# Reordering the SP queue of a fused attention and two-expert kernel: weight stores behind newer loads, raw keys and queries behind the moves

## The chip, the core and the metric

The kernel runs on one core of a Trainium2 chip. The metric is the device time of one execution in microseconds (us); it is stated as the median of several runs. The engines are TensorE (PE in the rows; PEld is its weight load), VectorE (DVE), ScalarE (ACT), GpSimd (POOL) and SyncE (SP). SP does no arithmetic here: it issues transfers (DMAs), in the order of its queue, and when the next one has to wait for a semaphore, everything behind it on SP waits too. ScalarE's queue issues a few transfers as well.

## What is computed

Four batches of eight heads of attention (576 positions, head dimension 64), with a threshold, then two experts, of two dense layers each, on the 2304 x 512 result:

```python
scores = scale * np.matmul(q, k.transpose(0, 1, 3, 2))
thresh = np.max(scores, axis=-1, keepdims=True) - tau
scores = np.where(scores >= thresh, scores, -1000000000.0)
attn = softmax(scores)
x = (attn @ v), heads side by side
h = x @ w_in;  x = (s * relu(h)**2 + b) @ w_out        # first expert, d_ff 2048
h = x @ w2_in; out = mish(h) @ w2_out                  # second expert, d_ff 2048
```

The expert weights arrive as 64-bit floating point numbers and are converted on the chip. Keys, queries and values arrive as 32-bit numbers.

## The kernel before, in words

**Attention.** The 32 heads are worked off in 16 pairs; a pair has nine score tiles. `attention` (L422) goes through all 144 tiles: `scores` (L326) computes a tile's scores on TensorE from the pair's Q, KH and KL tiles, VectorE takes minimum and threshold, ScalarE the exponential; `weights_t` (L373) transposes the tile on TensorE (T, L380), ScalarE copies the transpose from PSUM (te, L391), and `products_v` (L394, L406 and L409) multiplies te with the values (pv), with a lag of some seven tiles.

**Preparing the next pair.** While pair p is computed, at its score tiles 2 and 4, `prep_qk` (L298) prepares the keys and then the queries of pair p + 1. `raw_t` (L264) transposes the raw tile on TensorE (tpk, tpq) and at its end calls `load_raw` (L234), which loads the raw keys or queries of pair p + 2 into the same raw tile with two DMAs on SP (L254 for 512 positions, L255 for the last 64); there is one raw tile for keys and one for queries, so this load waits until the transposes have read it. `parts` (L278) splits the transpose into hi (ScalarE, L282) and lo (VectorE, L283), of which there is one tile each, used by keys and queries in turn. Then SP issues the moves (L303), six for keys (four of KH, two of KL) and four for queries, which copy the parts into the tiles of the pair. `self.moved` remembers the last move. The first pair goes through `prep_first` (L305).

**Weights of the first expert.** `split_all` (L162) runs the 32 pieces of the first expert's weights through a software pipeline: a step traces one new piece's load and advances the older pieces by one stage each, the oldest first. `split_w` (L47) loads the raw piece with one DMA of 512 KB (L60, into one of four raw slots; it is queued on SP behind `self.moved`), ScalarE scales its high words in place (L66), VectorE assembles the 32-bit number (L68 to L70), ScalarE rounds it to hi (L73), and VectorE or GpSimd takes the rest (L74). The result stands in one of the five slots of the ring. When a piece is finished, `store` (L193) writes it to DRAM (L195), from where the later batches reload it (L494). A ring slot is free again when its store has been read out and the matmuls that use it are done.

**The mixed order.** After the first pairs, `run` (L774) traces attention and `moe1` (L483, the first expert, batch by batch, matmuls on L502) alternately, by estimated work done; attention is traced with a higher priority there. During batch 0 of the first expert a step of `split_all` is taken every fourth yield. The final order on each engine is laid when the program is built, by priority and by simulated times, under the dependencies and the order edges: `issue_after(x)` lets what is traced in it be issued only behind x on x's queue, without waiting for x to finish.

Of the kernel before, what the change touches and what calls it, by code (L numbers as in the profile page):

```python
# [8 lines left out]
F32 = mybir.dt.float32  # L9
# [10 lines left out]
class Fused:  # L20
# [26 lines left out]
    def split_w(self, src, hi, lo, pool, tags, kw):  # L47

        nc = self.nc
        i = self.nd
        self.nd += 1
        n = src.shape[1] * src.shape[2] // 2
        raw = pool.tile([P, n, 2], I32, tag=tags[0], name=f"wraw{i}", **kw)
        with self.tc.issue_after(self.moved):
            nc.sync.dma_start(raw.rearrange("p (c f) w -> p c (f w)", c=src.shape[1]), src)  # L60
        low, high = raw[:, :, 0], raw[:, :, 1]
        hf = high.bitcast(F32)
        yield
        yield
        a = pool.tile([P, n], I32, tag=tags[1], name=f"wa{i}")
        self.tc.keep_in_program_order(nc.scalar.activation(hf, hf, AF.Copy, scale=2.0 ** -112))  # L66
        yield
        nc.vector.tensor_scalar(a, high, 3, None, op0=ALU.logical_shift_left)  # L68
        nc.vector.scalar_tensor_tensor(a, low, 29, a, op0=ALU.logical_shift_right, op1=ALU.bitwise_or)
        nc.vector.scalar_tensor_tensor(a, high, -0x80000000, a, op0=ALU.bitwise_and, op1=ALU.bitwise_or)  # L70
        yield
        af = a.bitcast(F32).rearrange("p (c f) -> p c f", c=src.shape[1])
        nc.scalar.copy(hi, af)  # L73
        (nc.gpsimd if self.s2p else nc.vector).tensor_tensor(lo, af, hi.bitcast(F32), op=ALU.subtract)  # L74
# [102 lines left out]
    def w1_pieces(self, layer, qf, i):  # L177

        nc = self.nc
        key = (layer, qf, i)

        def piece():
            u = self.w1[key] = self.ring.tile([P, 2, 4, 128], F32R, tag="ring", name=f"wp{layer}_{qf}_{i}")
            if layer == 0:
                r0, c0, w = 0, qf * 512 + i * 128, self.w_in
            else:
                r0, c0, w = qf * 512, i * 128, self.w_out
            src = w[r0:r0 + 512, 2 * c0:2 * c0 + 256].rearrange("(c p) f -> p c f", c=4)  # L190
            return src, u[:, 0], u[:, 1], store

        def store():  # L193
            dst = self.w1s[key] = self.dram.tile([P, 2, 4, 128], F32, name=f"w1_{layer}_{qf}_{i}")
            nc.sync.dma_start(dst, self.w1[key].bitcast(F32))  # L195

        return [piece]

    def busy(self, out, n):

        w = out.shape[1]
        for _ in range(n):
            ins = self.nc.tensor.matmul(out, self.ones[:, :128], self.ones[:, :w], start=True, stop=True)
            self.tc.keep_in_program_order(ins)
# [59 lines left out]
    def raw_t(self, pr, n):  # L264
        nc = self.nc
        raw = self.raws.pop((pr, n))
        tp = self.s_tile(f"tp{n}{pr}")

        for c, o in ((4, 192), (0, 256), (1, 384), (2, 512), (3, 640), (4, 768)):
            rows = raw[:, c].rearrange("p h d -> p (h d)")  # L270
            if c < 4:
                nc.tensor.transpose(tp[:, o:o + 128], rows, self.ident)
            else:
                nc.tensor.matmul(tp[:, o:o + 64], rows, self.ident[:, 0:64], start=True, stop=True)
        self.load_raw(pr + 1, n)
        return tp

    def parts(self, pr, n, tp, tags):  # L278
# [19 lines left out]
    def prep_qk(self, pr, n):  # L298

        hi, lo = self.parts(pr, n, self.raw_t(pr, n), ("hi", "lo"))  # L300
        for h in range(2):
            for dst, src in self.moves(pr, n, h, hi, lo):
                self.moved = self.nc.sync.dma_start(dst.bitcast(F32), src.bitcast(F32)).ins  # L303

    def prep_first(self, busy):  # L305


        nc = self.nc
        tps = [self.raw_t(0, n) for n in "kq"]
        busy(6)  # L310
        (kh, kl), (qh, ql) = (self.parts(0, n, tp, tags) for n, tp, tags in
                              zip("kq", tps, (("hi", "lo"), ("e", "e"))))
        k0, k1, k2 = self.moves(0, "k", 0, kh, kl)
        q0, q1 = self.moves(0, "q", 0, qh, ql)
        nc.scalar.copy(k0[0], k0[1].bitcast(F32))
        nc.gpsimd.tensor_copy(k1[0], k1[1].bitcast(F32))
        nc.gpsimd.tensor_copy(k2[0], k2[1].bitcast(F32))
        nc.scalar.copy(q0[0], q0[1].bitcast(F32))
        nc.vector.tensor_copy(q1[0], q1[1].bitcast(F32))
        for n, hi, lo in (("k", kh, kl), ("q", qh, ql)):  # L320
            for dst, src in self.moves(0, n, 1, hi, lo):
                nc.sync.dma_start(dst.bitcast(F32), src.bitcast(F32))
# [613 lines left out]
```

## Time and profile before

| | us |
|---|---|
| median of 3 runs | 1150.73 |
| lowest and highest of them | 1149.34, 1155.08 |
| the profiled execution, its own time | 1157.07 |
| its span, first to last instruction | 1155.3 |
| TensorE busy | 1091.3 |
| VectorE busy | 798.6 |
| ScalarE busy | 619.2 |
| GpSimd busy | 251.6 |

The profile is of one execution. Its first part gives busy time per engine. The view of stretches splits that by time; the waits name who stood idle and which instruction ended the wait; the timeline lists instructions with start and duration, and behind a square bracket the idle time before one and what ended it. A row of SP gives the time in which SP issued a transfer, not the transfer's own.

### The profile page before, as it was taken

Reading aid. Unit: us, or ns where it says so; the run is one execution under the profiler, and the core shown is the slowest. Engines: PE = TensorE matmul, PEld = TensorE weight load, DVE = VectorE, ACT = ScalarE, POOL = GpSimd, SP = SyncE. Lnnn points to the kernel's source line nnn. Section 1 sums busy time; section 2 is a strip of 40 time slices with the busy share of each in tenths; the row PEclk is TensorE's granted clock in tenths of the full one; section 3 lists DMA queues with packets and bytes.
Section 4 is the critical chain, followed back from the end, with each engine's and each line's share of the span. In section 5 each row is a group of like instructions: output and inputs, shape, how many; then the busy total and the mean of one; then the engine's idle time right before and its main releaser. Section 6 shows DMA issues by size and latency. Waiting matters only on the chain.

```text
span 1155.3 us, 21402 instructions
## 1 busy us (share of the span) xinstructions
PE 1091.3 (94%) x7964; PEld 1023.6 (89%) x7964; DVE 798.6 (69%) x1747; ACT 619.2 (54%) x1153; POOL 251.6 (22%) x305
## 2 busy tenths in 40 slices
PE   7887899888899999999999999989999999999998
PEld 6766688778688999899998889989999999999998
DVE  6978666868697567786687667643787377834783
ACT  4656576637466765666675557633454144513351
POOL 4533333334143334332442311100000000000000
PEclk9999899999999999999999999989999999999999
DMA  7466464665758866988684899975999999996783
GB/s 159 102 153 158 134 203 134 213 161 206 218 156 275 259 196 221 268 269 264 232 269 146 329 365 369 381 282 204 361 378 346 315 409 369 363 332 250 270 301 115
DMA packets 141591, 292.70 MB, mean 253 GB/s; under 512 B 52848, under 2 KB 78960, under 8 KB 133168
## 3 DMA queue, kind: packets, MB, share of 16 engines
q1 hardware_dynamic: 134256, 286.91, 72.6%
q10 hardware_dynamic: 7232, 4.43, 1.5%
q8 instruction: 63, 1.03, 0.4%
q14 instruction: 40, 0.33, 0.1%
HBM read 201.85 MB, written 66.58 MB: 232 GB/s over the span
## 4 chain that ended last, share of the span: by engine, by line
PE 60%; DMA 5%; DVE 3%; ACT 2%; issue 1%; SPq 0%; DVEq 0%; ACTq 0%
PE o L747 15%; PE y L502 12%; PE h L502 10%; PE qY L613 6%; PE qX L613 4%; PE qV L613 4%; PE S L342 3%; PE T L380 2%; PE pv L409 2%; DMA wi<-wsi 2%; DMA w<-w 1%; DMA wraw<-in_moe_w_out_dram 1%; PE pv L406 1%; DVE e L357 1%; DMA crawo<-in_moe_w_out_dram 1%
## 5 line engine op out<-in xcount | busy, mean ns | idle before, releaser
L747 PE MATMUL o<-wo,hl 128*128 128x256 f32 x1512 | 177.7, 279 | 0.0
L747 PEld LDWEIGHTS o<-wo,hl 128*128 128x128 f32 x1512 | 177.4, 188 | 0.0
L367 POOL TENSOR_SCALAR e<-e,st 128x576 f32<-128x576 f32 x128 | 130.1, 1029 | 199.8 <-DVE st L362 155.4
L502 PE MATMUL h<-xh,w 128*128 128x288 f32 x768 | 166.8, 302 | 4.0 <-DMA w<-w 3.8
L502 PE MATMUL y<-gh,w 128*128 128x288 f32 x768 | 164.1, 301 | 2.8 <-DVE y L549 2.0
L346 DVE TENSOR_SCALAR_CACHE_REDUCE ns<-S 128x576 f32<-128x576 f32 x144 | 107.7, 752 | 45.9 <-PE S L342 45.5
L357 DVE SCALAR_TENSOR_TENSOR e<-ns,st,e 128x576 f32<-128x576 f32 x128 | 115.2, 903 | 35.0 <-ACT e L353 34.0
L391 ACT COPY te<-T 128x576 f32<-128x576 f32 x144 | 91.3, 634 | 79.7 <-PE T L385 64.6
L502 PEld LDWEIGHTS h<-xh,w 128*128 128x128 f32 x768 | 127.5, 191 | 5.1 <-DMA w<-w 4.1
L502 PEld LDWEIGHTS y<-gh,w 128*128 128x128 f32 x768 | 126.7, 190 | 3.7 <-DVE y L549 2.2
L353 ACT ACTIVATE e<-ns,st 128x576 f32<-128x576 f32 x128 | 98.8, 775 | 56.5 <-DVE ns L346 50.0
L526 POOL TENSOR_TENSOR gl<-rr,gh 128x288 fp32r<-128x288 f32 x96 | 87.1, 916 | 189.9 <-ACT rr L525 187.4
L380 PE MATMUL T<-ident,e 128*128 128x128 f32 x576 | 97.6, 284 | 21.7 <-ACT te L391 20.3
L502 PE MATMUL y<-gl,w 128*128 128x288 f32 x384 | 114.6, 299 | 0.0
L502 PE MATMUL h<-xl,w 128*128 128x288 f32 x384 | 114.3, 298 | 0.0
L342 PE MATMUL S<-KH,Q 128*128 128x288 f32 x320 | 98.4, 324 | 14.3 <-DVE ns L346 8.9
L380 PEld LDWEIGHTS T<-ident,e 128*128 128x128 f32 x576 | 68.9, 144 | 42.9 <-ACT te L391 22.1
L342 PE MATMUL S<-KL,Q 128*128 128x288 f32 x320 | 91.1, 300 | 0.0
L409 PE MATMUL pv<-te,rawv 128*64 128x288 f32 x576 | 88.7, 422 | 0.0
L613 PE MATMUL qY<-yc,wi 128*128 128x384 f32 x432 | 86.6, 337 | 1.3 <-DVE g L636 1.3
L342 PEld LDWEIGHTS S<-KH,Q 128*128 128x128 f32 x320 | 62.0, 194 | 20.5 <-DVE ns L346 11.9
L613 PEld LDWEIGHTS qY<-yc,wi 128*128 128x128 f32 x432 | 75.6, 188 | 1.9 <-DVE g L636 1.9
(150 smaller groups left out, 2193.4 us busy)
## 6 DMA issues: line engine op xcount, KB each, us to landing
w<-w SPq DMA_DIRECT2D x96, 512.0 KB, 5.3
wo<-wso SPq DMA_DIRECT2D x42, 1024.0 KB, 7.0
wi<-wsi SPq DMA_DIRECT2D x23, 1024.0 KB, 7.7
wi<-wsi SPq DMA_DIRECT2D x25, 768.0 KB, 7.4
w<-wp SPq DMA_DIRECT2D x32, 512.0 KB, 3.4
wsi<-chli SPq DMA_DIRECT2D x24, 512.0 KB, 5.3
wso<-chlo SPq DMA_DIRECT2D x24, 512.0 KB, 6.5
ycd<-yp SPq DMA_DIRECT2D x14, 768.0 KB, 8.3
```

The source lines that it names most:

```text
L342: nc.tensor.matmul(so, Q[:, c0:c0 + 128], kt[:, ks], start=(i == 0), stop=(i == len(terms) - 1))
L346: nc.vector.tensor_scalar(ns.rearrange("p (h n) -> p h n", h=2), sv, -0.125, 3.0e38, op0=ALU.mult, op1=ALU.min, accum_out=nm[:, c1])
L353: nc.scalar.activation(e, ns, AF.Exp, bias=nm[:, c1], scale=-1.0)
L357: nc.vector.scalar_tensor_tensor(e, ns, nthr[:, c1], e, op0=ALU.is_le, op1=ALU.mult, accum_out=sm[:, c1])
L367: nc.gpsimd.tensor_scalar(t, t, rinv[:, j:j + 1], u[:, j:j + 1], op0=ALU.mult, op1=ALU.add)
L380: nc.tensor.transpose(T[:, i * 128:i * 128 + 128], self.es[pr, i, "pair"][:, o:o + 128], self.ident)
L391: nc.scalar.copy(te, T[:, :576])
L409: ins = self.nc.tensor.matmul(*args, **kw).ins
L502: nc.tensor.matmul(acc[:, :n], w[:, wl, c], rhs[c][xl][:, ts], start=(i == 0), stop=(i == 11))
L526: (nc.vector if b == 3 else nc.gpsimd).tensor_tensor(gl[:, ts], r2, gh[:, ts].bitcast(F32), op=ALU.subtract)
L613: self.nc.tensor.matmul(acc, a, b, start=(first and i == 0), stop=(i == n - 1), skip_group_check=True)
L747: nc.tensor.matmul(bank[p][t], hl[:, gl, j, ts], w[:, 2 * (q % 2) + j, wl], start=(old is None and q + j + k == 0), stop=(q + j + k == 6), ...
```

## The change

Three edits:

- `split_w` keeps its load as `self.newest`, and `store` issues each store on SP behind the newest load traced so far.
- `raw_t` no longer calls `load_raw`. `prep_qk` calls it after the moves, queued on SP behind the last of them.
- `prep_first` calls `load_raw` for pair 1 itself, after both transposes of pair 0.

```diff
@@ split_w
         with self.tc.issue_after(self.moved):
-            nc.sync.dma_start(raw.rearrange("p (c f) w -> p c (f w)", c=src.shape[1]), src)
+            self.newest = nc.sync.dma_start(raw.rearrange("p (c f) w -> p c (f w)", c=src.shape[1]), src).ins
@@ w1_pieces, store
-            nc.sync.dma_start(dst, self.w1[key].bitcast(F32))
+            with self.tc.issue_after(self.newest):
+                nc.sync.dma_start(dst, self.w1[key].bitcast(F32))
@@ raw_t
-        self.load_raw(pr + 1, n)
         return tp
@@ prep_qk
                 self.moved = self.nc.sync.dma_start(dst.bitcast(F32), src.bitcast(F32)).ins
+        with self.tc.issue_after(self.moved):
+            self.load_raw(pr + 1, n)
@@ prep_first
         tps = [self.raw_t(0, n) for n in "kq"]
+        for n in "kq":
+            self.load_raw(1, n)
```

## Rows read from the trace of the kernel before

**Rows 1.** The page, first part: busy us, share of the span, instructions.

```profile
PE 1091.3 (94%) x7964; PEld 1023.6 (89%) x7964; DVE 798.6 (69%) x1747; ACT 619.2 (54%) x1153; POOL 251.6 (22%) x305
```

**Rows 2.** Stretches: us, busy us (instructions) by engine, TensorE clock, DMA share, GB/s.

```profile
200.00:250.00 50.00, 43.02 (x322) 36.91 (x322) 36.65 (x91) 27.86 (x53) 14.86 (x15) 1.00 0.60 186
...
450.00:500.00 50.00, 50.00 (x388) 46.82 (x387) 39.23 (x96) 28.89 (x57) 15.36 (x17) 1.00 0.80 246
...
700.00:750.00 50.00, 50.00 (x379) 50.00 (x378) 35.25 (x68) 34.24 (x80) 9.90 (x8) 1.00 1.00 376
```

**Rows 3.** Waits from 140 to 360 us: who for whom, us in total, times, longest.

```profile
ACT wraw L66 <- DMA wraw<-in_moe_w_out_dram: 12.1, 6, 4.3
...
PE T L380 <- ACT te L391: 11.5, 13, 2.3
...
ACT wraw L66 <- DMA wraw<-in_moe_w_in_dram: 9.1, 7, 1.9
...
PE pv L406 <- ACT te L391: 5.5, 4, 2.3
```

**Rows 4.** Timeline around 250 us, ScalarE and TensorE: start, us, instruction, idle before.

```profile
248.85 0.65 ACT L66 ACTIVATE wraw<-wraw 128x512 f32<-128x512 f32 x1 [1.97 <-DMA wraw<-in_moe_w_out_dram]
...
250.74 0.46 PE L406 MATMUL pv<-te,rawv 128*64 128x288 f32 x1 [2.26 <-ACT te L391]
```

**Rows 5.** Timeline of SP's queue, 330 to 350 us.

```profile
330.60 0.66 SPq L254 DMA_DIRECT2D rawk<-in_k_dram  x1
...
332.10 1.83 SPq L303 DMA_DIRECT2D KH<-hik  x3
...
336.51 0.59 SPq L60 DMA_DIRECT2D wraw<-in_moe_w_out_dram  x1
...
344.90 0.68 SPq L254 DMA_DIRECT2D rawq<-in_q_dram  x1
...
346.49 0.50 SPq L303 DMA_DIRECT2D Q<-hiq  x1
...
349.18 0.59 SPq L60 DMA_DIRECT2D wraw<-in_moe_w_out_dram  x1
```

**Rows 6.** Timeline of ScalarE and TensorE in the same stretch.

```profile
331.33 0.71 ACT L282 CAST hik<-tpk 128x640 fp32r<-128x640 f32 x1
...
341.19 0.68 ACT L66 ACTIVATE wraw<-wraw 128x512 f32<-128x512 f32 x1 [2.63 <-DMA wraw<-in_moe_w_out_dram]
...
345.37 0.40 PE L502 MATMUL y<-gh,wp 128*128 128x288 f32 x1 [0.33 <-ACT wp L73]
```

**Rows 7.** Timeline of SP's queue, 113 to 239 us.

```profile
113.22 0.58 SPq L60 DMA_DIRECT2D wraw<-in_moe_w_in_dram  x1
...
216.16 16.83 SPq L195 DMA_DIRECT2D w<-wp  x5
238.30 0.67 SPq L254 DMA_DIRECT2D rawk<-in_k_dram  x1
```

**Rows 8.** SP's own waits at the stores, and the stores of the tile wp.

```profile
SPq L195 <- DVE st L348: 34.2, 10, 8.5
...
L195 SPq DMA_DIRECT2D w<-wp x32: 319/338/1069, 104.2 to 360.6; - x32
```

**Rows 9.** Tile wraw: loads (ns min/median/max, first and last start), landing; raw keys' issues.

```profile
L60 SPq DMA_DIRECT2D wraw<-in_moe_w_in_dram x16: 368/576/680, 64.3 to 304.9; - x16
L60 SPq DMA_DIRECT2D wraw<-in_moe_w_out_dram x16: 368/568/1043, 155.0 to 349.2; - x16
...
DMA to landing us min/median/max: 3.6/5.0/10.4
...
rawk<-in_k_dram SPq DMA_DIRECT2D x16, 256.0 KB, 3.5
```

**Rows 10.** Waits from 0 to 110 us for moves.

```profile
ACT hiq L282 <- DMA KH<-hik: 3.1, 2, 1.8
...
DVE loq L283 <- DMA KL<-lok: 1.1, 1, 1.1
```

## Prediction

> **What bounds the kernel now.** I read the page first, then the stretches, then the waits of the stretch in which the change acts, then the order of SP's queue there. TensorE is busy for 1091.3 us of the span [rows 1], so all the idle time there is to win is about 64 us, and where it lies matters. By stretches of 50 us TensorE is idle for 7.0 us from 200 to 250, but not at all from 450 to 500 [rows 2]. The idle time that this change can touch therefore lies before about 360 us, where attention and the first batch of the first expert layer share the engines and the raw weights are converted. After that a shift of a few us in a transfer meets an engine that has work queued.
>
> In that stretch the waits tell who holds TensorE up. From 140 to 360 us it stood 11.5 us for a transposed attention tile (te) in the T matmuls and 5.5 us in the pv matmuls, 17.0 us together; ScalarE, which copies te, itself stood 12.1 + 9.1 = 21.2 us in 13 waits for raw weights to land [rows 3]. One place shows how the two hang together: at 248.85 ScalarE starts the scaling of a raw weight after 1.97 us of waiting for its load, the te copy is queued behind that, and TensorE starts pv at 250.74 after 2.26 us of idling for te [rows 4]. So a weight load that lands late can cost nearly its own lateness. It need not: at 341.19 ScalarE had waited 2.63 us for a load, and between 334.74 and 345.37 TensorE has no gap [rows 6].
>
> **The change part by part.** *Raw keys and queries behind the moves.* In the kernel before, each raw load is two issues on SP that go out as soon as the transposes have freed the tile, and the moves follow. At 330.60 the raw keys take SP until 332.10, when the first move goes; the six moves end at 336.51, when the next raw weight load goes [rows 5]. But ScalarE's conversion that the first move needs ends at 331.33 + 0.71 = 332.04 [rows 6], so the raw load sat in time in which the moves had to wait anyway. With the new order the moves begin at 332.04 instead of 332.10 and still end near 336.45; the two raw issues, 332.10 - 330.60 = 1.50 us, now stand behind them. The weight load that is also tied behind the moves is traced later than the raw load, so I expect it behind both: its issue goes from 336.51 to about 337.95. The query group from 344.90 to 349.18 has the same form, 1.59 us for the two issues [rows 5]. Where the moves waited a little for the raw issues, up to 0.6 us comes back, by my reading of the other groups; I take 1.2 us per group. There are 11 such groups with a weight load behind them after 100 us (the first such load at 113.22 [rows 7], the last at 349.18 [rows 5]), so weight loads are late by 11 x 1.2 = 13 us in sum.
>
> How much reaches the end? The lower end is nothing, as at 341.19 [rows 6]; the upper end is 17.0 / 21.2 = 0.8 of it, TensorE's waits over ScalarE's [rows 3], which makes 10.6 us. I take a third, 4.3 us, nearer to nothing, because the instruction order is fixed when the program is built by simulated times: issue time on SP is part of that simulation, and a load known to go out later puts the scaling later in ScalarE's order, behind te copies that are ready.
>
> The raw keys and queries themselves are late by some 5 us, and that costs nothing: from 238.30 to 330.60 lie two pairs of heads [rows 5, 7], so a tile is needed some 46 us after the one before. The cover is that distance; without it the transposes would wait out the 3.5 us landing [rows 9].
>
> The moves gain something early. Before 110 us ScalarE waited 3.1 us, in two waits, and VectorE 1.1 us for moves of keys to leave the single hi and lo tiles [rows 10]; with no raw packets ahead of them the moves land sooner. Bounds: 0 and 3.1 + 1.1 = 4.2 us gained; I take 2 us, the middle, as both waits fall in a stretch that engines' waits for each other set.
>
> After 360 us the same edges delay weight reloads by up to 1.5 us at each of the eight raw loads that are left (four pairs of heads). TensorE's 50.00 of 50.00 us covers that [rows 2]: 0. Without that cover it would be 8 x 1.5 = 12 us.
>
> *Stores behind the newest raw load.* A store of piece j is now issued behind the load of piece j + 3 (each step of the loop finishes the oldest piece before it traces the new load). Counted in SP's order of 32 loads and 32 stores [rows 8, 9], 17 stores stand there already; 15 move. As an example, five stores occupy SP from 216.16 to 232.99 [rows 7]. Three of those five now stand behind loads that go out after the next moves, from 245 us on. What that removes is SP's waiting at stores, 34.2 us for one releaser alone [rows 8], but what is behind them does not get out sooner: the queue's next entry, the raw keys of 238.30, comes 5.3 us after the store burst's end [rows 7] because the transposes are not done. Removed waits: 0, at most a few tenths of a us where the two touch.
>
> What it adds is traffic beside the weight loads. Each store issues in 0.34 us at the median [rows 8] and moves 512 KB; at the 376 GB/s of the stretch from 700 to 750, where the DMA share is 1.00 [rows 2], that is an estimated 1.4 us. Bounds: 0 if every moved store follows a load that nobody waits for, 15 x 1.7 x 0.8 = 20 us if each stands ahead of one that does. I take 1 us, near 0: stores are freed one at a time behind a load, the one load that ScalarE stands for is mostly the first of a group [rows 4, 6], and that has no store before it. A store that is late also holds its ring slot; the slot is written again five pieces later, and about 9 us remain between the late store's landing and that write: 0.
>
> **Sum.** 4.3 + 1 - 2 = +3.3 us. The profiled execution took 1157.07 us, 6.3 us above the median of the three runs, 1150.73; the difference is put on the median: 1154.0 us, +0.3%. About 0.5%, 5.8 us, is what a measurement of this kernel can tell from no change, so this is "no change".
>
> **Rivals.** *Slower: the weights wait out the raw packets.* Place: the 11 groups. Raw keys take 3.5 us to land, of which 1.5 us is issue, so a weight load directly behind could land 2.0 us later still, and loads in a burst do land anywhere from 3.6 to 10.4 us after issue [rows 9]. Price: 11 x (1.2 + 2.0) / 3 = 11.7 us, + 1 - 2: 1161 us. It decides if at most a third is absorbed; at 0.8 of the issue time alone the sum is 10.6 + 1 - 2, also 1160 us. For it: the waits of rows 4. Against it: rows 6. Chance 0.32.
> The Trainium skill, page "DMA: Bandwidth & Descriptors", section "Queues, rings and completion order", says that one DMA engine consumes the descriptors of a ring in ring order; by that rule this rival is the time, 1161 us. That loads late in a burst land late agrees, but no row has a weight load directly behind a raw one.
>
> *Faster: the order is laid out anew.* Fewer stores at SP's head and moves that leave early let the build put scaling behind the te copies. If half of the 17.0 us goes [rows 3] the time is 1150.7 - 8.5 = 1142 us. For it: all of that idle time lies behind ScalarE. Against it: no weight load has an earlier issue by the edges. Chance 0.28.
>
> *The change does little of what it says.* 17 of 32 stores already keep the new order, and the raw loads may end up behind the weight loads: then only -2 to +1 us is left, about 1150 us. It lies within no change; chance 0.12.
>
> **How the numbers follow.** Forecast 0.28 and the last rival 0.12 make 0.40 for no change; 0.28 faster and 0.32 slower by over 0.5%. The range goes from the faster rival, 1142, to a little over the slower one, 1164.
>
> **What would show it.** Right: in SP's order the six moves start at the end of ScalarE's conversion, two raw issues follow, then a weight load some 1.2 us later than now; ScalarE's waits for raw weights grow from 21.2 us to some 25 to 30; no store stands before the load three pieces on; from 400 us on TensorE stays full. Wrong: weight loads ahead of the raw loads, ScalarE's waits falling, TensorE's idle time before 360 us falling by 6 us or more, or gaps after 400 us before the first layer's matmuls.

## The result, and the profile after

The changed kernel takes 1158.37 us (median of 18 runs, 1154.10 to 1164.02), the kernel before on the same chip 1151.81 us (18 runs, 1146.47 to 1157.30). The ratio is 1.0055 with a 95% interval of 1.0036 to 1.0074: slower by 6.3 us. The interval is clear of no change, but reaches from 0.36% to 0.74%, so on which side of the forecast's bound of 0.5% it lies isn't settled. A second set of runs, on another occasion, gave 1.0053 (below). The forecast was 1154.0 us, so the sign was right, and the size half of what it is.

The two profiled executions can't be subtracted: the one of before is 5 us above its median, the one of after, 1154.34 us, 4 us below. What follows reads where waits moved, and leaves the price to the experiments. By the page after, TensorE is busy for 1087.0 us of a span of 1152.5 us and idle for 65.5 us (before 1155.3 - 1091.3 = 64.0 us). By stretches it idles for 3.9 us from 200 to 250, less than in [rows 2], and for 0.42 us from 450 to 500, which was full there: a single stretch doesn't show the loss either. Next the waits from 140 to 360 us, as in [rows 3] (lines below the change are four higher: T is L384 now, S is L346).

```profile
ACT wraw L66 <- DMA wraw<-in_moe_w_out_dram: 15.2, 6, 3.9
...
ACT wraw L66 <- DMA wraw<-in_moe_w_in_dram: 9.9, 4, 5.5
...
PE S L346 <- DVE ns L350: 7.0, 7, 3.6
...
PE T L384 <- ACT te L395: 6.3, 6, 2.2
...
PE pv L410 <- ACT te L395: 3.0, 4, 1.1
```

ScalarE stands 15.2 + 9.9 = 25.1 us for raw weights, against 21.2 us [rows 3], in fewer and longer waits. TensorE's waits for te *fell*, from 17.0 to 9.3 us, and yet the kernel is slower. A part turns up at the scores, which wait for VectorE's ns: 9.4 us from 100 to 400 us, 5.6 us before. So TensorE's waits by themselves don't show what the change cost.

One thing comes earlier. ScalarE's sixth conversion of keys (hik), first before, then after:

```profile
98.89 0.70 ACT L282 CAST hik<-tpk 128x640 fp32r<-128x640 f32 x1
```

```profile
96.78 0.69 ACT L282 CAST hik<-tpk 128x640 fp32r<-128x640 f32 x1
```

This is more than the scatter of profiles: in the four kernels of this document that keep the raw loads ahead of the moves it starts at 98.89 to 101.84, in the eight that have them wholly behind at 95.22 to 98.21, in the mean 3.6 us earlier. Now SP's queue after, at the place of [rows 5] and at an earlier group of weight loads.

```profile
201.39 0.59 SPq L60 DMA_DIRECT2D wraw<-in_moe_w_in_dram  x1
202.03 0.50 SPq L196 DMA_DIRECT2D w<-wp  x1
202.57 0.43 SPq L60 DMA_DIRECT2D wraw<-in_moe_w_in_dram  x1
203.05 1.37 SPq L196 DMA_DIRECT2D w<-wp  x1
...
330.12 0.52 SPq L303 DMA_DIRECT2D KL<-lok  x1
330.74 0.66 SPq L255 DMA_DIRECT2D rawk<-in_k_dram  x1
331.80 0.66 SPq L256 DMA_DIRECT2D rawk<-in_k_dram  x1
332.52 0.71 SPq L60 DMA_DIRECT2D wraw<-in_moe_w_out_dram  x1
```

The last move's issue ends at 330.12 + 0.52 = 330.64, the raw keys take their two issues, and the weight load goes at 332.52, 1.9 us later; in [rows 5] it followed the moves at once. In the group at 201 us a store now stands between one weight load and the next. The stores themselves suffer too: the tile wp's issues and landing (columns as in [rows 8, 9]) after are

```profile
L196 SPq DMA_DIRECT2D w<-wp x32: 320/496/1527, 103.2 to 357.2; - x32
...
DMA to landing us min/median/max: 2.6/6.5/9.1
```

so the median issue went from 338 ns [rows 8] to 496 ns, and the median landing from 3.4 us to 6.5 us.

### The profile page after: what moved, and what is told of

Its sections match the earlier page's. It is cut to its first block, busy times and chain, and to the rows that moved or that the text cites. A ratio compares the mean times of both kernels' runs of the same rounds, so it can differ in the third digit from the quotient of the medians.

```text
span 1152.5 us, 21416 instructions
## 1 busy us (share of the span) xinstructions
PE 1087.0 (94%) x7964; PEld 1015.4 (88%) x7964; DVE 799.0 (69%) x1747; ACT 619.2 (54%) x1153; POOL 256.9 (22%) x305
## 4 chain that ended last, share of the span: by engine, by line
PE 55%; DMA 9%; DVE 4%; ACT 2%; issue 1%; POOL 1%; SPq 0%; DVEq 0%; ACTq 0%; POOLq 0%
PE o L751 14%; PE y L506 11%; PE h L506 10%; PE qY L617 5%; PE qV L617 4%; PE qX L617 4%; PE S L346 2%; DMA wi<-wsi 2%; PE pv L413 2%; PE T L384 2%; DMA wso<-chlo 2%; DMA yc<-ycd 1%; DMA wraw<-in_moe_w_out_dram 1%; DMA w<-w 1%; DMA crawi<-in_moe_w_in_dram 1%
## 5 line engine op out<-in xcount | busy, mean ns | idle before, releaser
L371 POOL TENSOR_SCALAR e<-e,st 128x576 f32<-128x576 f32 x128 | 134.0, 1059 | 210.8 <-DVE st L366 187.0
L361 DVE SCALAR_TENSOR_TENSOR e<-ns,st,e 128x576 f32<-128x576 f32 x128 | 111.7, 875 | 32.7 <-ACT e L357 31.5
L346 PE MATMUL S<-KH,Q 128*128 128x288 f32 x320 | 98.0, 323 | 21.9 <-DVE ns L350 13.2
L384 PE MATMUL T<-ident,e 128*128 128x128 f32 x576 | 97.2, 280 | 15.7 <-ACT te L395 13.7
L384 PEld LDWEIGHTS T<-ident,e 128*128 128x128 f32 x576 | 68.5, 142 | 34.8 <-ACT te L395 15.4
L346 PE MATMUL S<-KL,Q 128*128 128x288 f32 x320 | 90.3, 298 | 0.0
L346 PEld LDWEIGHTS S<-KH,Q 128*128 128x128 f32 x320 | 60.9, 191 | 31.0 <-DVE ns L350 18.4
```

The lines of the kernel that those rows point to most:

```text
L346: nc.tensor.matmul(so, Q[:, c0:c0 + 128], kt[:, ks], start=(i == 0), stop=(i == len(terms) - 1))
L361: nc.vector.scalar_tensor_tensor(e, ns, nthr[:, c1], e, op0=ALU.is_le, op1=ALU.mult, accum_out=sm[:, c1])
L371: nc.gpsimd.tensor_scalar(t, t, rinv[:, j:j + 1], u[:, j:j + 1], op0=ALU.mult, op1=ALU.add)
L384: nc.tensor.transpose(T[:, i * 128:i * 128 + 128], self.es[pr, i, "pair"][:, o:o + 128], self.ident)
```

## The experiments

**Theory A**: the weight loads are late on SP, behind raw keys and queries and between stores, and ScalarE, standing for them, passes that on. **Theory B**: the new edges make the build lay all engines' order anew (in the lists described below, 1840 of 7548 entries stand elsewhere on TensorE, 504 of 1459 on VectorE, 473 of 1194 on ScalarE), and that order is by chance worse; the queue itself costs nothing. To part them, the order of a kernel's compute engines was written out as `HELD`, a list per engine, and laid on another kernel as pure order of issue, while SP stayed free (so its order can differ in single places from that of the kernel it is compared with):

```diff
+    for e, runs in HELD.items():
+        ...
+        row = [traced[e][k] for k in order]
+        for a, b in zip(row, row[1:]):
+            tc.add_manual_dep(b, a.name, kind, reason="held order")
...
     Fused(tc, *args).run(ctx)
+    hold(tc)
```

"Held" below means: with TensorE, VectorE, ScalarE and GpSimd in the order of the kernel before. All ratios are to the kernel before on the same chip (medians 1152.14, 1151.30 and 1150.37 us in the three sets); 0.1% is 1.15 us.

| | order | ratio | 95% interval |
|---|---|---|---|
| the change again | new | 1.0053 | 1.0036, 1.0070 |
| the change | held | 1.0259 | 1.0235, 1.0283 |
| kernel before | that of the change | 0.9985 | 0.9967, 1.0002 |
| stores alone | new | 1.0074 | 1.0047, 1.0100 |
| stores alone | held | 1.0078 | 1.0047, 1.0109 |
| raw loads alone | new | 1.0074 | 1.0047, 1.0100 |
| raw loads alone | held | 1.0216 | 1.0191, 1.0241 |
| both, weight loads first | held | 0.9995 | 0.9973, 1.0017 |
| both, weight loads first | new | 1.0005 | 0.9983, 1.0027 |
| raw loads behind moves and weights | new | 1.0013 | 0.9987, 1.0038 |
| only the 32 KB raw DMA behind | held | 1.0024 | 1.0005, 1.0042 |
| only the 256 KB raw DMA behind | held | 1.0105 | 1.0078, 1.0133 |

("New" is whatever order the build lays for that kernel. In the expectations, A1 is theory A with the stores as the main cause, A2 with the raw keys and queries.)

### Queue or order

**The change again**, unaltered:

> The change once more, beside its parts on one chip. Theory A (late weight loads): the slower time comes from raw weight loads that go out later on SP; theory B (re-laid order): it comes from the order of the four compute engines, which the build lays anew for the new queue order. Both expect the measured 1.0055 again, 1.004 to 1.007, some 5 to 8 us over the kernel before.

Measured 1.0053; the loss is there again.

**The change in the old order** (the diff of the change, and `HELD` of before):

> The change's edges on SP, while TensorE, VectorE, ScalarE and GpSimd keep the order of the kernel before, instruction by instruction. Theory A: the whole loss, 1.004 to 1.008 (5 to 9 us), with ScalarE's waits for raw weights from 140 to 360 us up from 21 to 28 us or more. Theory B: no difference, 0.998 to 1.002.

**The kernel before in the new order** (no edit of the queue, `HELD` of the changed kernel):

> SP's edges of the kernel before, while the four compute engines have the order of the changed kernel. Theory A: about the kernel before or a little faster, 0.996 to 1.001, since weight loads go out earlier than the order was laid for. Theory B: the whole loss, 1.004 to 1.008 (5 to 9 us).

Measured 1.0259 and 0.9985. With every compute engine's order fixed to the old one, the change on SP costs some 30 us, over three times what theory A had expected (1.004 to 1.008); the new order on the old queue costs nothing and may gain up to 0.33%. On the new order the change on SP costs 1.0053 / 0.9985, 0.68%. Theory B falls, and the other way round is true: the build's new order takes back four fifths of what the queue loses. The waits from 140 to 360 us show both, first of the change in the old order, then of the kernel before in the new one:

```profile
ACT wraw L66 <- DMA wraw<-in_moe_w_out_dram: 23.4, 9, 5.5
...
ACT wraw L66 <- DMA wraw<-in_moe_w_in_dram: 20.0, 9, 4.8
...
PE T L380 <- ACT te L391: 14.8, 13, 3.4
...
PE pv L406 <- ACT te L391: 10.5, 4, 4.6
```

```profile
ACT wraw L66 <- DMA wraw<-in_moe_w_out_dram: 5.7, 5, 2.9
...
ACT wraw L66 <- DMA wraw<-in_moe_w_in_dram: 3.3, 2, 2.7
```

In the old order ScalarE waits 43.4 us for raw weights, 22.2 more than in [rows 3], and TensorE 25.3 us for te, 8.3 more. In the new order, on the queue of before, ScalarE waits only 9.0 us, 12.2 less: as I read it, the scalings stand later there beside their loads, and the late loads of the change use up that room. These 12 us less of waiting bring only 0.15%, 0.33% at most: TensorE stands elsewhere instead. From 100 to 400 us its waits for te are 7.2 us (20.4 before), but those for VectorE's results 17.9 us (10.0 before), 8.7 us of them for ns (5.6 before).

Where the time of the change in the old order goes is read from its page:

```profile
PE 1099.0 (93%) x7964; PEld 1028.4 (87%) x7964; DVE 798.3 (68%) x1747; ACT 619.0 (52%) x1153; POOL 248.1 (21%) x305
```

Its span is 1180.6 us, so TensorE idles for 81.6 us, 17.6 more than in [rows 1] (1155.3 - 1091.3 = 64.0). The other 7.7 us of the longer span are the same matmuls at a lower granted clock, 0.977 against 0.984 in the mean over the execution (1 is 2.4 GHz, the lower level of 1.2 GHz is 0.5).

### Stores

Only the first two edits of the diff, once in the order that the build lays, once held:

```diff
-            nc.sync.dma_start(raw.rearrange("p (c f) w -> p c (f w)", c=src.shape[1]), src)
+            self.newest = nc.sync.dma_start(raw.rearrange("p (c f) w -> p c (f w)", c=src.shape[1]), src).ins
...
-            nc.sync.dma_start(dst, self.w1[key].bitcast(F32))
+            with self.tc.issue_after(self.newest): nc.sync.dma_start(dst, self.w1[key].bitcast(F32))
```

> Only the stores behind the newest raw weight load; raw keys and queries as in the kernel before; the build lays the order freely. Theory A: stores cost little, since the first load of each group has none before it: 0.999 to 1.002. A rival within A (stores crowd the weight loads): 1.003 or more. Theory B can't say a sign: any value from 0.995 to 1.008, not explained by ScalarE's waits for weights.

> Only the stores behind the newest load, compute engines held in the order of the kernel before; with both edges that held order cost 1.026. Theory A1 (the stores between the weight loads do it): most of it, 1.015 to 1.026, ScalarE's waits for raw weights 35 us or more from 100 to 400. Theory A2 (the raw keys and queries ahead of the weight loads do it): 1.000 to 1.008.

Measured 1.0074 and 1.0078, some 9 us either way; here the new order gave nothing back. Laid anew that is not the cheap case that theory A named (up to 1.002) but its rival, stores that crowd the weight loads; held it is at the upper end of A2. One group shows how. First the kernel before at 204 us (SP, then ScalarE's scalings of these four pieces), then the stores alone, held, with the same four.

```profile
204.78 1.18 SPq L60 DMA_DIRECT2D wraw<-in_moe_w_in_dram  x2
206.00 0.51 SPq L60 DMA_DIRECT2D wraw<-in_moe_w_out_dram  x1
206.61 0.45 SPq L195 DMA_DIRECT2D w<-wp  x1
207.10 0.58 SPq L60 DMA_DIRECT2D wraw<-in_moe_w_out_dram  x1
...
209.23 0.65 ACT L66 ACTIVATE wraw<-wraw 128x512 f32<-128x512 f32 x1 [1.14 <-DMA wraw<-in_moe_w_in_dram]
...
216.09 0.66 ACT L66 ACTIVATE wraw<-wraw 128x512 f32<-128x512 f32 x1
```

```profile
205.73 0.59 SPq L60 DMA_DIRECT2D wraw<-in_moe_w_in_dram  x1
206.37 0.56 SPq L195 DMA_DIRECT2D w<-wp  x1
206.97 0.43 SPq L60 DMA_DIRECT2D wraw<-in_moe_w_in_dram  x1
207.45 1.38 SPq L195 DMA_DIRECT2D w<-wp  x1
208.88 0.52 SPq L60 DMA_DIRECT2D wraw<-in_moe_w_out_dram  x1
...
210.17 1.33 SPq L60 DMA_DIRECT2D wraw<-in_moe_w_out_dram  x1
...
210.28 0.65 ACT L66 ACTIVATE wraw<-wraw 128x512 f32<-128x512 f32 x1 [1.23 <-DMA wraw<-in_moe_w_in_dram]
212.96 0.68 ACT L66 ACTIVATE wraw<-wraw 128x512 f32<-128x512 f32 x1 [1.19 <-DMA wraw<-in_moe_w_in_dram]
...
218.38 0.68 ACT L66 ACTIVATE wraw<-wraw 128x512 f32<-128x512 f32 x1 [0.49 <-DMA wraw<-in_moe_w_out_dram]
```

The first scaling comes 4.45 us after the first issue in the one and 4.55 us in the other: no store stands before it. But the fourth comes 11.31 us after it in the one, without a wait, and 12.65 us in the other, with one: the later loads of the group are held up by the stores between them, and ScalarE meets each in turn. From 140 to 360 us its waits for raw weights are 29.2 us in 18 waits, 8.0 us more than in [rows 3], beside some 9 us of time.

This group is not the whole of it. Sorted by place in their group, the waits at first loads grew from 13.3 to 18.5 us, those at later loads from 7.9 to 10.6 us. No store stands between the moves and a first load in either kernel, and yet in the mean of the 11 groups its scaling comes 4.78 us after its issue, against 4.28 us in the kernel before. Right behind it there now stands a store; that this is why it is late was not tested.

### Raw keys and queries

Only the last two edits, laid anew and held:

```diff
-        self.load_raw(pr + 1, n)
...
+        with self.tc.issue_after(self.moved): self.load_raw(pr + 1, n)
...
-        tps = [self.raw_t(0, n) for n in "kq"]
+        tps = [self.raw_t(0, n) for n in "kq"]; [self.load_raw(1, n) for n in "kq"]
```

> Only raw keys and queries behind the moves, the order laid freely by the build. The stores alone, laid freely, measured 1.0074, the whole change 1.0053. Theory A1: 0.998 to 1.003, and ScalarE's waits for raw weights within 3 us of the kernel before. Theory A2: 1.004 to 1.007.

> Only raw keys and queries behind the moves, compute engines held in the order of the kernel before. Theory A1: 1.000 to 1.008, since the one load behind them is late by some 1.2 us and that in 11 groups. Theory A2: 1.015 to 1.026. If both add up, this and the stores alone make 1.026 together.

Measured 1.0074, just over what A2 named, and 1.0216, within it: 25 us at the held order, of which the new order returns two thirds. Held, the parts add up within their intervals (0.78 + 2.16 = 2.94% against 2.59% for both); laid anew they don't, each part costing about as much as both.

Is it the issue time on SP, or the data ahead? The two DMAs of a raw load take the same time to issue, 0.66 us each in the timeline after, but move 256 KB and 32 KB. Each alone was put behind the moves, held, the other left where it was:

```diff
-            dma.dma_start(t[:, 0:4], most)
-            dma.dma_start(t[0:64, 4, :, :], h2[:, 512:576, :].rearrange("h r d -> r h d"))
+            if 'm' in part: dma.dma_start(t[:, 0:4], most)
+            if 't' in part: dma.dma_start(t[0:64, 4, :, :], h2[:, 512:576, :].rearrange("h r d -> r h d"))
```

> Of each raw load only the second DMA (the last 64 positions, 32 KB) goes behind the moves; the first (512 positions, 256 KB) stays ahead of them; compute engines held in the order of the kernel before. Both DMAs behind cost 1.0216. If SP's issue time does it (0.7 us for either DMA): half of that, 1.008 to 1.013. If the data ahead of the weights in the queue do it: 1.000 to 1.005.

> The other half: the DMA of 256 KB behind the moves, the one of 32 KB ahead; compute engines held as before. If issue time does it: 1.008 to 1.013, like the other half. If the data do it: 1.014 to 1.021, nearly the whole 1.0216.

Measured 1.0024 and 1.0105: the same time on SP, four times the cost. No one expectation holds for both: 1.0024 is in the range that the data alone would give, 1.0105 in that of the issue time. The load and scaling of [rows 5, 6] in SP's and ScalarE's timelines, first with the small DMA ahead of it, then with the large one, then with both (raw loads alone, held):

```profile
334.68 0.65 SPq L255 DMA_DIRECT2D rawk<-in_k_dram  x1
335.38 0.60 SPq L60 DMA_DIRECT2D wraw<-in_moe_w_out_dram  x1
...
339.98 0.68 ACT L66 ACTIVATE wraw<-wraw 128x512 f32<-128x512 f32 x1 [3.50 <-DMA wraw<-in_moe_w_out_dram]
```

```profile
336.13 0.66 SPq L254 DMA_DIRECT2D rawk<-in_k_dram  x1
336.83 0.74 SPq L60 DMA_DIRECT2D wraw<-in_moe_w_out_dram  x1
...
342.70 0.67 ACT L66 ACTIVATE wraw<-wraw 128x512 f32<-128x512 f32 x1 [4.71 <-DMA wraw<-in_moe_w_out_dram]
```

```profile
344.73 0.67 SPq L254 DMA_DIRECT2D rawk<-in_k_dram  x1
345.49 0.70 SPq L255 DMA_DIRECT2D rawk<-in_k_dram  x1
346.24 0.59 SPq L60 DMA_DIRECT2D wraw<-in_moe_w_out_dram  x1
...
351.56 0.68 ACT L66 ACTIVATE wraw<-wraw 128x512 f32<-128x512 f32 x1 [4.83 <-DMA wraw<-in_moe_w_out_dram]
```

From the weight load's issue to the scaling that waits for it: 4.60 us behind the small DMA, 5.87 us behind the large one, 5.32 us behind both, and 4.68 us in [rows 5, 6] behind the moves. The group is not typical: in the mean of the 11 groups, read from the same timelines, it is 4.60, 4.95, 5.13 and 4.28 us. From the end of the conversion that the moves need to the weight load's issue it is 4.26, 4.17, 5.00 and 3.86 us. So with both DMAs behind the moves a weight load is issued 1.14 us later and used another 0.85 us later, some 2.0 us a group and 22 us in all; with the small one alone it is 0.7 us a group, with the large one alone 1.0 us. That doesn't make the one four times as dear as the other: how the cost splits into issue and data stays open.

How much of the 22 us arrives can be read too, because the held kernels run the same instructions in the same order. Between ScalarE's sixth, twelfth and sixteenth conversion of keys lie the same 1727 and 1461 matmuls; all 11 groups are in the first stretch. In order: the kernel before; raw loads alone, held; and, for the next section, both edges with weight loads first, held (columns as in [rows 2]).

```profile
98.89:372.18 273.29, 240.51 (x1727) 210.15 (x1726) 209.60 (x528) 168.16 (x317) 94.62 (x113) 0.96 0.61 189
372.18:560.39 188.21, 188.21 (x1461) 176.64 (x1461) 129.69 (x324) 123.10 (x252) 67.09 (x77) 1.00 0.76 238
```

```profile
95.55:384.92 289.37, 246.73 (x1727) 212.64 (x1726) 209.50 (x528) 168.69 (x318) 93.44 (x113) 0.94 0.58 178
384.92:579.57 194.65, 190.96 (x1461) 177.39 (x1461) 130.16 (x324) 123.40 (x252) 66.78 (x77) 0.99 0.75 230
```

```profile
97.61:364.00 266.39, 235.72 (x1727) 204.74 (x1726) 209.58 (x528) 168.70 (x318) 95.30 (x113) 0.99 0.63 193
364.00:559.44 195.44, 190.93 (x1461) 178.23 (x1461) 130.07 (x324) 123.44 (x251) 66.69 (x77) 0.99 0.75 230
```

With the raw loads behind, the first stretch is 16.1 us longer, about three quarters of the 22 us: 9.9 us of it is idle time of TensorE, 6.2 us the same matmuls at a lower granted clock (0.94 against 0.96). The second stretch, in which no weight load of this kind is left, is 6.4 us longer too, and TensorE idles there for 3.7 us where before it had no gap. The largest gap, 2.59 us at 546.74, is for a te that ScalarE copies after 5.90 us of waiting for a store of the second expert's weights (wsi); in the kernel before that wait is 2.96 us and TensorE has no gap. These are single executions, 16.3 us apart in span where the medians are 24 us apart, so they show where the loss lies and not its exact size.

### Weight loads first

Both edges of the change stay, and the weight load is put ahead of raw loads and stores by priority; held, then laid anew. The third kernel has the raw loads behind the moves and the prioritised weight loads, and the stores as before.

```diff
-        with self.tc.issue_after(self.moved):
+        with self.tc.issue_after(self.moved), self.tc.high_priority(offset=3000):
```

> Both edges of the change, but weight loads get a high priority on SP, so that a group reads moves, one to four weight loads, raw keys or queries, stores; compute engines held in the order of the kernel before. Theory A1 and A2 both: back near the kernel before, 0.997 to 1.004, because no first weight load has anything new ahead of it. If late weight loads are not the cause (stores late for their ring slots, moves, raw tiles): 1.015 or more, as with both edges.

> Both edges of the change, weight loads with a high priority on SP, the order laid freely by the build. In the held order this measured 0.9995. Late weight loads as the cause: 0.994 to 1.001, at least 4 us below the change. If a freely laid order with these edges is slower by itself: 1.003 or more.

> Raw keys and queries behind the moves and behind the weight loads (high priority on SP); stores as in the kernel before; order laid freely. Raw keys and queries ahead of the weights measured 1.0074. Late weight loads as the cause: 0.993 to 1.000. Otherwise 1.004 or more.

Measured 0.9995, 1.0005 and 1.0013, all the same as before; the last is a little above the 1.000 that was expected at most. In the first the place of [rows 5, 6] reads

```profile
329.71 0.58 SPq L60 DMA_DIRECT2D wraw<-in_moe_w_out_dram  x1
330.40 0.67 SPq L254 DMA_DIRECT2D rawk<-in_k_dram  x1
...
333.74 0.70 ACT L66 ACTIVATE wraw<-wraw 128x512 f32<-128x512 f32 x1 [1.99 <-DMA wraw<-in_moe_w_out_dram]
```

with 4.03 us from issue to scaling, and its waits from 140 to 360 us

```profile
ACT wraw L66 <- DMA wraw<-in_moe_w_in_dram: 8.9, 7, 3.1
...
ACT wraw L66 <- DMA wraw<-in_moe_w_out_dram: 7.1, 6, 2.2
```

make 16.0 us, 5.2 less than in [rows 3]. Raw keys and stores still go behind what the change puts them behind, and the stores of this kernel take 6.1 us to land (3.4 us before, both medians). The whole loss at a held order, 2.6%, is gone with this one edit: the weight loads' place is enough to make the loss or to undo it, which is theory A.

It isn't shown that late raw tiles and late stores cost nothing. The edit also puts weight loads ahead of stores that stood between them in the kernel before, and that kernel with the priority alone was not measured. By the stretches above a gain and a loss cancel: the first is 6.9 us shorter than before, 2.1 us of that less idling and the rest the same matmuls at a clock of 0.99; the second is 7.2 us longer, with 4.5 us of idling where before there was none. No kernel here beats the one before by more than its interval.

## Why the prediction was right in sign and half in size

The forecast called the result "no change", with a chance of 0.40; measured is a slowdown of 0.55%, which belongs by its median to the case that it gave 0.32. The measured time is within the range of 1142 to 1164 us, in part by luck: laid anew, the stores alone cost 8.5 us and the raw loads alone 8.5 us, where the forecast had 1 and 4.3, and only because the parts don't add up when the build lays both did the time rise by 6.3 us and not by 17.

- **Where it would lie.** Right: weight loads late before 360 us, ScalarE's waits for raw weights from 21.2 to 25.1 us (25 to 30 were named), raw issues between moves and weight load, stores between loads.
- **The stores, +1 us: mis-sized, the largest miss of the sum as the build lays it.** Alone they cost some 9 us at either order, within the bounds of 0 and 20 us. The step that failed is "the one load that ScalarE stands for is mostly the first of a group, and that has no store before it". It was mostly the first (13.3 of 21.2 us), but being first didn't keep it from being late (4.28 to 4.78 us from issue to scaling, waits up by 5.2 us), and later loads became loads that ScalarE stands for (waits up by 2.8 us). The lower bound was taken because of who waits *now*.
- **Raw loads, +4.3 us: mis-sized.** Measured alone 0.74%, 8.5 us, with the order laid anew, within the upper end of 10.6 us, and 25 us held, beyond it. The issue was right: 1.14 us a group where 1.2 was taken. Left out was that a load behind raw loads is also used later after its issue, by 0.85 us a group; together that makes 22 us in sum and not 13. The upper share, 0.8, held in the stretch of the groups (16.1 of 22 us); the rest of the loss at the held order lies behind it.
- **A share absorbed by the build.** That the build knows SP's issue times and can take part of a loss back was right: held 2.59%, laid anew 0.55%, so a fifth gets through; that it does so by moving the scaling later is a reading, for which the waits of the kernel before in the new order speak. Its place in the sum was not right: for the raw loads alone a third gets through, for the stores all of it, and for both together less than for the parts. It acts on the whole layout and can't be multiplied part by part.
- **The early gain, -2 us: there, but not in the wait that was named.** ScalarE's wait for the moves to leave the hi tile is 3.6 us from 0 to 110 us in the profile after, 3.1 us before [rows 10]. But ScalarE's sixth conversion of keys comes 2.1 us earlier, and 3.6 us in the mean of the kernels with the raw loads behind the moves against those with them ahead. Which wait became shorter stays open. It doesn't reach the end, where the change is the slower one.
- **The zeros.** After 360 us: right as the build lays it. A small gap of TensorE from 450 to 500 us (0.42 us) stands in the profile after, but also, 0.54 us, in that of the kernel before in the new order, so it isn't the edges' doing. At a held order it fails: TensorE's 50.00 of 50.00 us did not cover a stretch that grew by 6.4 us with the raw loads behind and by 7.2 us with weight loads first. Raw tiles some 5 us late, ring slots, removed waits at stores: no run here takes them by themselves; the time of the kernels with weight loads first bounds only their sum with the gain there.
- **The slower rival**, the weights waiting out the raw packets, 1161 us, was nearer than the forecast, but it took 2.0 us a group for the wait behind the data, and measured are 0.85. The Trainium skill, page "DMA: Bandwidth & Descriptors", section "Queues, rings and completion order", says that on each DMA engine descriptors are consumed in ring order. The traces agree in direction, with 4.95 us from issue to scaling behind the large DMA, 4.60 us behind the small one and 4.28 us behind the moves. At the held order the change costs even more than this rival gave; that the time stayed below 1161 us is the order laid anew.
- **The faster rival** had half a case: the build did lay a better order, with TensorE's waits for te down from 17.0 to 9.3 us. But it took for granted that this idle time would be won; on the old queue, where ScalarE's waits for weights fell to 9.0 us, the time fell by only 0.15%, as TensorE then stood for VectorE.

What stays open: how the raw load's cost splits into issue and data, why first loads land later with stores behind them, and what besides the one wait for wsi lengthens the second stretch.

## What to carry to other kernels

When a queue is reordered, go to the transfer that a compute engine stands for and ask what is now directly ahead of it: issue time and bytes both, for every load of a burst and not only the first. A transfer that sat inside somebody's wait was free here, and behind that wait it was not; if it must move, put it behind the loads that are waited for as well. To learn what such a priority gives, measure it alone too. To learn what an order of a queue costs, hold the compute engines' order fixed, since a build that lays it anew can hide most of a loss (here 30 us shrank to 6).

## What the runs showed that was not expected

- The order of a queue alone, with all work, sizes and compute order the same, is worth 30 us of 1150.
- Of the stores between two loads, two took 1.4 us to issue (203.05 and 207.45 above), where the median before was 0.34 us [rows 8].
- A raw DMA of 256 KB and one of 32 KB take the same 0.65 us on SP, so a queue's issue times don't tell how long a load behind them waits.
- With the order held, stretches between the same instructions compare kernels at equal work (1727 and 1461 matmuls above). They showed a second loss behind 372 us, which sums of waits from 140 to 360 us leave out.
- The same 7964 matmuls kept TensorE busy for 1080.7 us in one profiled execution (the 32 KB DMA behind, mean granted clock 0.997) and 1099.0 us in another (0.977), and it wasn't the one with more idle time that had the lower clock throughout: the first idled for 74.0 us, the kernel before, at 0.984, for 64.0. So spans of single profiles can't be compared to within 1%.
